# Spacing the tasks that read DMA-added weight blocks, and letting the next item's tasks go ahead

## The chip, the cores and the metric

The kernel runs on one core of a Trainium2 chip. The metric is device time in microseconds (us), the median of several executions, lower being better. TensorE is called PE in the profile, its weight loads PEld, VectorE DVE, ScalarE ACT, GpSimd POOL and SyncE SP.

## The reference

Three layers follow each other. The input is four batches of 576 tokens with 512 features.

- Attention: 8 heads of width 64, with a mask that is causal by blocks of 64 tokens.
- A mixture of 8 experts, all of them applied to all tokens: for each expert `relu(x @ w1[e]) @ w2[e]`, weighted by a router matrix `P` that is normalised over rows and columns eight times in turn. The hidden width of an expert is 1024.
- A gated layer: `(silu(x @ w_gate) * (x @ w_val)) @ w_out` with a hidden width of 1536.

All inputs and outputs are 32-bit floats; the weights of the last layer reach the kernel as pairs of words and are put together on the chip.

## The kernel before, in words

Each large product is done as seven half-size products instead of eight (a scheme of Strassen's kind), and each operand as a high and a low 16-bit part. So each weight tile of 512 by 512 needs seven operands: three are splits of its own 256-wide blocks or their negatives (W11, W21, W22), four are splits of sums of blocks (T1 to T4). The splits run on ACT (the high part, L173) and DVE (the low part, L174). The sums are not made by an engine that computes: a DMA issued from POOL adds one block onto another in place (L292).

The experts make 16 units of one w1 tile and one w2 tile each (u = 0 to 15). Units 0 and 1 run for the first token blocks beside attention; the second tile of these two needs no sums. From u = 2 on, the main stage runs one unit after the other over five token blocks (four of 256 pairs of tokens, one of 128). A unit has 63 *slots*: in each slot PE does six matmuls (or twelve of half width) of the unit's first product (`products_in`, L543) and six of a second product (`products_out`, L651) of an earlier block. The counter `clock[0]` goes up by one in each such step of `products_in`, by `tick()`, and nowhere else before the last stage.

Weights of later units are prepared in the background. An *item* is one weight tile (or, for the last layer, a quarter of one), with a list of *tasks*. `Background.step` takes the next task of the current item, if there is one and it may go. The item of a weight tile has four tasks that find block maxima (L376, with a negation on ACT at L348), an exchange of the maximum over partitions by way of PE, and then the tasks of `sum_tasks`:

- t0 splits W11. t1 finishes it, adds block 01 onto block 00 and splits W21. t2 finishes it, adds 11 onto 10 and splits W22. t3 finishes it and adds 11 onto 01.
- one `gap`, a task that does nothing
- t5 splits T1 from block 00 and adds 00 onto 10. t6 finishes it and adds 00 onto 11.
- two gaps
- t8 splits T3 from block 01. t9 splits T4 from block 10. t10 splits T2 from block 11. One more task finishes it.

In the main stage `background()` calls `step` up to twice a slot: once when the work left is over 4 tasks behind an even pace that would end at slot 58 of the unit, a second time when it is over 9 behind. A unit's items are the two tiles of the unit that follows, and a share of the last layer's quarters, in the order `share[:-2] + [i1] + share[-2:] + [i2]`. A last-layer tile is prepared in four quarter items, the fourth of which also has the sum tasks; its operands are written to DRAM for later. `bg.until((u, 0))` and `bg.until((u, 1))` run what is left of a tile at once, with `force`, when its unit's products are about to need it.

Beside attention another such object, `w0`, does units 0 and 1. There `step` is called 0.53 times for each of the three parts of an attention step, and no item is loaded ahead of the current one (`Background(0)`). The products of units 0 and 1 start there when the first batch has been through attention, in `first_part`: it calls `w0.until((0, 0))`, then the products of unit 0 on block 0 (14 half products, one for each two parts of an attention step), then `w0.finish()`, which runs all that is left of `w0` at once, then the products of unit 1.

A task's first entry is the number of buffers it needs free, or a function that says whether it may go; the maximum's exchange already used such a function.

Of the kernel before, what the change touches and what calls it, by code (L numbers as in the profile page):

```python
# [25 lines left out]
W11, W21, W22, T4, T1, T2, T3 = range(7)  # L26
# [4 lines left out]
def attention_moe_glu_kernel(  # L31
# [187 lines left out]
    clock = [0]  # L219
    places = Places(0)  # L220

    class Background:
# [14 lines left out]
        def step(self, force=False):  # L237
            self.turn += 1
            if not self.now:
                if not self.items:  # L240
                    return False
                if not self.loaded:
                    self.load(1)
                if not self.loaded or self.turn < self.loaded[0] and not force:
                    return False
                self.now.extend(self.items.popleft()[2])
                self.loaded.popleft()
            self.load(self.ahead)
            n, t, *kind = self.now[0]
            self.light = kind == [0]  # L250
            if not places.spare(n, force):
                return False
            self.now.popleft()
            if t is not None:
                t()
            if kind == [2] and not self.now and self.loaded and self.turn >= self.loaded[0]:
                n, t, *kind = self.items[0][2][0]
                if kind == [0] and places.spare(n):
                    self.loaded.popleft()
                    self.now.extend(self.items.popleft()[2])  # L260
                    self.now.popleft()
                    t()
            elif self.light and self.loaded and self.turn >= self.loaded[0]:
                tasks = self.items[0][2]
                if tasks[0][2:] == (1,) and places.spare(tasks[0][0]):
                    self.light = False
                    t = tasks.pop(0)[1]
                    if not tasks:
                        self.items.popleft()
                        self.loaded.popleft()  # L270
                    if t is not None:
                        t()
            return True

        def finish(self):
            while self.now or self.items:
                assert self.step(True), "no place left"
# [3 lines left out]
                assert self.step(True), "no place left"  # L281


    def sum_tasks(b, sp, name, flip):

        los = {}

        def add(o, x):
            nc.gpsimd.dma_start(o, x, accum_op=ALU.add)  # L292

        def up(o, src, minus=False):
            los[o] = sp(o, src, minus)

        def low(o, *gone):
            los.pop(o)()
            places.give(*gone)

        def t0():
            up(W11, b[0][0])

        def t1():
            low(W11)
            add(b[0][0], b[0][1])
            up(W21, b[1][0], True)

        def t2():
            low(W21)  # L310
            add(b[1][0], b[1][1])
            up(W22, b[1][1])

        def t3():
            low(W22)
            add(b[0][1], b[1][1])

        def t5():
            up(T1, b[0][0], True)
            add(b[1][0], b[0][0])  # L320

        def t6():
            low(T1)
            add(b[1][1], b[0][0])

        def t8():
            up(T3, b[0][1])

        def t9():
            low(T3, b[0][1])  # L330
            up(T4, b[1][0], True)
            places.give(b[0][0])

        def t10():
            low(T4, b[1][0])
            up(T2, b[1][1], flip)

        gap = (0, None, 0)
        return (
            [(1, t0, 0), (1, t1), (1, t2), (0, t3)]  # L340
            + [gap] * 1
            + [(1, t5, 0), (0, t6)]
            + [gap] * 2
            + [(1, t8, 0), (1, t9), (1, t10), (0, lambda: low(T2, b[1][1]))]
        )

    def minus(x):
# [4 lines left out]
    def expert_items(u):  # L352
# [8 lines left out]
        for i, W in enumerate((W1, W2)):  # L361
# [42 lines left out]
            if i == 1 and u < 2:  # L404

                def plain_sp(r, c, g=g, sp=sp):
                    sp((r, c), g["b"][r][c])()
                    places.give(g["b"][r][c])

                tasks += [(1, lambda r=r, c=c, f=plain_sp: f(r, c)) for r in range(2) for c in range(2)]  # L410
            else:
                tasks += sum_tasks(g["b"], sp, f"w{i}_{u}", i == 1)
# [6 lines left out]
    def glu_items(name, src, rawp):  # L419
# [66 lines left out]
        for t, r, c in quads:  # L486
            if (r, c) == (0, 0):
                b = [[None, None], [None, None]]
            cur = {}

            def last(cur=cur, b=b, r=r, c=c):
                mx(b, r, c)

            def first(cur=cur, b=b, q=(t, r, c)):
                exponent(cur, b, *q)
                if q[1:] == (1, 0):
                    minus(b[0][1])
                elif q[1:] == (1, 1):
                    minus(b[1][0])

            tasks = [(1, first, 0)]
            tasks += [(0, lambda cur=cur: (shift(cur), sign(cur))), (0, lambda cur=cur: mantissa(cur)), (0, last, 2)]
            if (r, c) == (1, 1):
                tasks[-1] = (0, lambda last=last, t=t: (last(), begin(t)))
                tasks += [(0, None, 0), (lambda force: across_made(g["r"])(force), lambda t=t: end(t))]
                tasks += sum_tasks(b, lambda o, src, minus=False, t=t: sp(t, o, src, minus), f"g{name}_{t}", name == "o")
            items.append((0, lambda cur=cur, q=(t, r, c): load(cur, *q), tasks))
# [1237 lines left out]
```

## Time and profile before

| | |
|---|---|
| time, median of 3 runs | 2194.89 us (2191.09 to 2196.18) |
| time of the profiled execution | 2203.99 us |
| its span, first to last instruction | 2202.2 us |
| PE busy | 2001.1 us, 91% |
| DVE, ACT, POOL busy | 72%, 62%, 32% |
| mean granted TensorE clock | 0.96 |
| L292, the adding DMAs | 195, of 256 KB each |

The span holds three stages: attention with units 0 and 1 up to about 385 us, the expert units up to about 1790 us, the last layer after that. An even pace of matmuls at full clock with no idle time would be the floor of the two latter. A busy PE says less than it seems, since its busy time also grows where the clock is halved.

### The profile page before, as it was taken

How to read it: one execution, taken by the hardware profiler on the slowest of the kernel's cores; microseconds unless marked ns; L12 is line 12 of the kernel's file. 1: busy time of each engine (PE TensorE's matmuls, PEld its weight loads, DVE VectorE, ACT ScalarE, POOL GpSimd, SP SyncE). 2: the span in 40 equal slices, each digit the busy share in tenths (PEclk: the TensorE clock that was granted, in tenths of full speed). 3: DMA queues.
4: the chain of work that ended last, by engine and by line, in shares of the span. 5: the costliest groups of instructions: out<-in, count | busy, mean ns of one | idle time of the engine just before them, and what ended most of it. 6: DMA issues, size and time to landing. Idle time of an engine off the chain costs nothing.

```text
span 2202.2 us, 47643 instructions
## 1 busy us (share of the span) xinstructions
PE 2001.1 (91%) x18378; PEld 1696.4 (77%) x18378; DVE 1596.5 (72%) x3583; ACT 1366.3 (62%) x2901; POOL 708.0 (32%) x1003
## 2 busy tenths in 40 slices
PE   6789899799989999898998988999888988999997
PEld 3356667688877888777887877888777887888887
DVE  6887774677777787776876767777776787666766
ACT  5666665467676677666776666677666556544442
POOL 4544343203333343333433333343333122100000
PEclk8889999899999999999999999999999999999999
DMA  6343331527887888878888797878879110210211
GB/s 170 104 121 96 106 88 48 148 54 149 173 183 151 171 158 171 185 144 174 157 167 178 145 182 146 176 148 161 186 146 202 40 45 1 57 46 17 62 40 49
DMA packets 180787, 272.22 MB, mean 124 GB/s; under 512 B 18512, under 2 KB 72784, under 8 KB 180560
## 3 DMA queue, kind: packets, MB, share of 16 engines
q0 software_dynamic: 78624, 143.17, 38.5%
q1 hardware_dynamic: 101936, 126.01, 18.7%
q8 instruction: 144, 2.36, 0.4%
q14 instruction: 83, 0.68, 0.1%
HBM read 90.98 MB, written 24.38 MB: 52 GB/s over the span
## 4 chain that ended last, share of the span: by engine, by line
PE 38%; DMA 17%; DVE 12%; issue 8%; ACT 6%; POOL 2%; POOLq 0%; ACTq 0%; DVEq 0%; SPq 0%
DMA wr<-wr 9%; PE abc_m_b L543 7%; PE m_o_b L651 6%; PE m_o_ac L651 5%; PE abc_m_c L543 3%; PE abc_v_b L543 3%; PE m_go_b L651 3%; PE abc_g_b L543 3%; PE m_go_ac L651 2%; PE abc_m_a L543 2%; DMA f_v<-f_v 2%; DMA f_g<-f_g 2%; DVE m_t L710 1%; DVE m_h L183 1%; PE abc_v_c L543 1%
## 5 line engine op out<-in xcount | busy, mean ns | idle before, releaser
L543 PEld LDWEIGHTS <-w 128*128 128x128 f16 x6720 | 620.0, 100 | 185.0 <-issue 111.4
L651 PEld LDWEIGHTS <-m_h 128*128 128x128 f16 x5292 | 521.0, 99 | 77.2 <-issue 11.6
L543 PE MATMUL abc_m_b<-xs,w 128*128 128x256 f16 (+1 forms) x3840 | 490.7, 269 | 71.5 <-DVE m_t L565 33.0
L1433 POOL DMA_DIRECT2D acc<-ev x351 | 340.4, 1098 | 549.7 <-ACT ev L1440 447.9
L651 PE MATMUL m_o_b<-w,m_h 128*128 128x256 f16 x3024 | 407.1, 274 | 5.9 <-ACT ev L1440 5.6
L651 PE MATMUL m_o_ac<-w,m_h 128*128 128x256 f16 x2268 | 320.7, 279 | 3.1 <-ACT ev L1440 3.1
L543 PE MATMUL abc_m_c<-xs,w 128*128 128x256 f16 (+1 forms) x1920 | 235.7, 267 | 22.9 <-ACT m_r L779 21.0
L173 ACT ACTIVATE w<-wr,ws 128x512 f16<-128x512 f32 x210 | 149.4, 720 | 123.1 <-DMA wr<-wr 109.0
L174 DVE SCALAR_TENSOR_TENSOR w<-wr,ws,w 128x512 f16<-128x512 f32 x210 | 156.9, 752 | 94.4 <-ACT w L173 94.1
L292 POOL DMA_DIRECT2D wr<-wr x150 | 147.5, 990 | 228.1 <-DMA wr<-wr 57.2
L1440 ACT ACTIVATE ev<-m_o_b,pe 128x256 f32<-128x256 f32 x351 | 161.6, 475 | 58.1 <-PE m_o_b L651 53.1
L183 DVE TENSOR_TENSOR m_h<-m_t,m_h 128x512 f16<-128x512 f32 (+1 forms) x210 | 132.9, 634 | 35.0 <-ACT m_h L689 34.8
L1440 ACT ACTIVATE ev<-m_o_ac,pe 128x256 f32<-128x256 f32 (+1 forms) x234 | 134.3, 579 | 36.9 <-PE m_o_ac L651 35.8
L682 ACT ACTIVATE m_h<-m_t 128x512 f16<-128x512 f32 (+1 forms) x210 | 120.5, 582 | 36.1 <-DVE m_t L580 18.5
L689 ACT CAST m_h<-m_t 128x512 f16<-128x512 f32 (+1 forms) x210 | 122.0, 581 | 16.7 <-DVE m_t L710 16.4
L686 DVE SCALAR_TENSOR_TENSOR m_h<-m_t,m_h 128x512 f16<-128x512 f32 (+1 forms) x210 | 131.1, 633 | 1.1 <-ACT m_h L682 0.7
L543 PEld LDWEIGHTS <-gg_w 128*128 128x128 f16 x1260 | 114.2, 98 | 21.4 <-issue 9.3
L1002 POOL TENSOR_SCALAR e<-e,r 128x64 f32<-128x64 f32 (+2 forms) x144 | 78.9, 555 | 159.8 <-DVE r L997 100.6
L651 PEld LDWEIGHTS <-g_h 128*128 128x128 f16 x1134 | 111.8, 99 | 19.6 <-issue 5.4
L543 PEld LDWEIGHTS <-gv_w 128*128 128x128 f16 x1260 | 114.4, 98 | 13.3 <-issue 1.2
L543 PE MATMUL abc_m_a<-xs,w 128*128 128x256 f16 (+1 forms) x960 | 119.3, 265 | 0.0
L691 POOL TENSOR_TENSOR g_h<-g_t,g_h 128x512 f16<-128x512 f32 (+1 forms) x15 | 16.0, 1069 | 250.8 <-ACT g_h L689 250.8
(319 smaller groups left out, 3454.8 us busy)
## 6 DMA issues: line engine op xcount, KB each, us to landing
acc<-ev POOLq DMA_DIRECT2D x351, 256.0 KB, 5.3
wr<-wr POOLq DMA_DIRECT2D x150, 256.0 KB, 4.0
wr<-in_w_dram SPq DMA_DIRECT2D x128, 256.0 KB, 4.7
st<-hl SPq DMA_DIRECT2D x48, 144.0 KB, 3.6
raw_g<-in_w_gate_dram SPq DMA_DIRECT2D x12, 512.0 KB, 5.1
raw_v<-in_w_val_dram SPq DMA_DIRECT2D x12, 512.0 KB, 5.4
raw_o<-in_w_out_dram SPq DMA_DIRECT2D x12, 512.0 KB, 4.8
scr_g<-gg SPq DMA_DIRECT2D x21, 256.0 KB, 3.6
```

The costliest lines, as they stand in the source:

```text
L173: nc.scalar.activation(hi, src, AF.Copy, scale=s)
L174: return lambda: nc.vector.scalar_tensor_tensor(lo, src, s, hi, op0=ALU.mult, op1=ALU.subtract)
L183: nc.vector.tensor_sub(lo, src, hi)
L292: nc.gpsimd.dma_start(o, x, accum_op=ALU.add)
L543: nc.tensor.matmul(ps[:, f], W[o][:, sh, k, f * P : (f + 1) * P], xs[:, o, mh, k, c0 : c0 + n], start=x not in begun, stop=True, skip_grou ...
L651: nc.tensor.matmul(ps, h[o][:, sh, k, ii * P : (ii + 1) * P], W[o][:, mh, k], start=o in (X11, X12) and k == 0 and j == 0, stop=True, skip ...
L682: nc.scalar.activation(hi, src, AF.Relu)
L686: nc.vector.scalar_tensor_tensor(lo, src, 0.0, hi, op0=ALU.max, op1=ALU.subtract)
L689: nc.scalar.copy(hi, src)
L1002: nc.gpsimd.tensor_scalar(et[c][:, :n], et[c][:, :n], g["r"][:, c : c + 1], 1.0, op0=ALU.mult, op1=ALU.mult)
L1433: nc.gpsimd.dma_start(acc[:, x], e, accum_op=ALU.add)
L1440: nc.scalar.activation(e[:, cols], ps, AF.Copy, scale=p)
```

## The change

Every task that reads a sum of blocks now may go only when `clock[0]` has moved on by six since the DMA that adds to its block was issued in the program (t5 waits for block 00, t8 for 01, t9 for 10, t10 for 11), unless it is forced. The three gaps go away. Where the next task of the current item may not yet go, and is one with such a function, `step` tries the first task of the next item instead, if that item has been loaded long enough, the task is not its last, and it needs no such function itself.

```diff
@@ Background.step
             if not places.spare(n, force):
-                return False
+                return callable(n) and self.ahead_of(self.items[0][2] if self.loaded and self.turn >= self.loaded[0] else ())
@@ Background
+        def ahead_of(self, tasks):
+
+            if len(tasks) < 2 or callable(tasks[0][0]) or tasks[0][1] is None or not places.spare(tasks[0][0]):
+                return False
+            n, t, *kind = tasks.pop(0)
+            self.light = kind == [0]
+            t()
+            return True
@@ sum_tasks
+    DMA_SLOTS = 6
...
+        added = {}
         def add(o, x):
             nc.gpsimd.dma_start(o, x, accum_op=ALU.add)
+            added[id(o)] = clock[0]
+
+        def summed(r, c):
+
+            return lambda force: (force or clock[0] >= added[id(b[r][c])] + DMA_SLOTS) and places.spare(1)
...
-        gap = (0, None, 0)
         return (
             [(1, t0, 0), (1, t1), (1, t2), (0, t3)]
-            + [gap] * 1
-            + [(1, t5, 0), (0, t6)]
-            + [gap] * 2
-            + [(1, t8, 0), (1, t9), (1, t10), (0, lambda: low(T2, b[1][1]))]
+            + [(summed(0, 0), t5, 0), (0, t6)]
+            + [(summed(0, 1), t8, 0), (summed(1, 0), t9), (summed(1, 1), t10), (0, lambda: low(T2, b[1][1]))]
         )
```

## Rows read from the trace of the kernel before

**Rows 1.** Page, chain of work that ended last, shares of the span by line.

```profile
DMA wr<-wr 9%; PE abc_m_b L543 7%; PE m_o_b L651 6%; PE m_o_ac L651 5%; PE abc_m_c L543 3%; PE abc_v_b L543 3%; PE m_go_b L651 3%; PE abc_g_b L543 3%; PE m_go_ac L651 2%; PE abc_m_a L543 2%; DMA f_v<-f_v 2%; DMA f_g<-f_g 2%; DVE m_t L710 1%; DVE m_h L183 1%; PE abc_v_c L543 1%
```

**Rows 2.** Waits, 481.61 to 1710.91 us: total us, times, longest.

```profile
ACT w L173 <- DMA wr<-wr: 103.9, 66, 4.1
PEld L543 <- issue: 93.6, 55, 5.8
...
ACT go L173 <- DMA f_o<-f_o: 20.1, 10, 4.9
...
ACT gg L173 <- DMA f_g<-f_g: 20.0, 11, 4.7
...
ACT gv L173 <- DMA f_v<-f_v: 18.6, 9, 4.7
```

**Rows 3.** Windows: units 2, 3, 5, 8, 10, 12 of thirteen, and all.

```profile
core 0: us, PE busy (x) PEld busy (x) DVE busy (x) ACT busy (x) POOL busy (x), PEclk, DMA share, GB/s
481.61:569.59 87.98, 83.69 (x798) 74.26 (x796) 67.08 (x138) 70.26 (x141) 32.94 (x38) 1.00 0.76 146
569.59:663.10 93.51, 85.94 (x798) 75.39 (x797) 70.43 (x139) 64.55 (x131) 35.84 (x42) 0.96 0.86 174
...
763.09:847.27 84.18, 83.54 (x806) 75.15 (x806) 67.27 (x139) 63.98 (x129) 32.88 (x38) 1.00 0.82 157
...
1041.13:1125.67 84.54, 83.68 (x806) 75.15 (x806) 67.33 (x139) 64.11 (x129) 32.91 (x38) 1.00 0.82 158
...
1222.51:1327.57 105.06, 90.68 (x802) 77.94 (x800) 73.41 (x151) 66.52 (x135) 36.72 (x42) 0.94 0.81 166
...
1426.89:1514.05 87.16, 85.14 (x806) 76.05 (x806) 67.35 (x139) 64.20 (x129) 32.94 (x38) 0.98 0.78 151
...
481.61:1710.91 1229.30, 1127.59 (x10423) 990.39 (x10421) 909.85 (x1836) 853.10 (x1713) 458.67 (x526) 0.97 0.83 165
```

**Rows 4.** Timeline of ACT in unit 9: start, duration, [idle before <- releaser].

```profile
1153.89 0.72 ACT L173 ACTIVATE gv<-f_v,gs_v 128x512 f16<-128x512 f32 x1 [1.27 <-DMA f_v<-f_v]
...
1160.35 0.72 ACT L173 ACTIVATE gv<-f_v,gs_v 128x512 f16<-128x512 f32 x1 [2.05 <-DMA f_v<-f_v]
1163.05 0.72 ACT L173 ACTIVATE gv<-f_v,gs_v 128x512 f16<-128x512 f32 x1 [1.98 <-DMA f_v<-f_v]
```

**Rows 5.** Timeline of PE just after.

```profile
1165.55 1.44 PE L543 MATMUL abc_m_b<-xs,w 128*128 128x256 f16 x6 [3.68 <-ACT abc_m_a L560]
1166.78 1.48 PE L651 MATMUL m_o_ac<-w,m_h 128*128 128x256 f16 x6
...
1171.71 0.82 PE L651 MATMUL m_o_b<-w,m_h 128*128 128x256 f16 x6
```

**Rows 6.** Timeline of POOL in the same sum: adds of t1, t3, t5, t6.

```profile
1150.38 0.86 POOL L292 DMA_DIRECT2D f_v<-f_v  x1 [1.25 <-DVE gv L174]
...
1154.40 0.86 POOL L292 DMA_DIRECT2D f_v<-f_v  x1 [0.81 <-DMA f_v<-f_v]
1157.10 0.86 POOL L292 DMA_DIRECT2D f_v<-f_v  x1 [1.84 <-DMA f_v<-f_v]
1160.94 0.86 POOL L292 DMA_DIRECT2D f_v<-f_v  x1 [2.98 <-PE abc_m_c L543]
```

**Rows 7.** Page, DMA issues: count, size, median us from issue to landing.

```profile
wr<-wr POOLq DMA_DIRECT2D x150, 256.0 KB, 4.0
```

**Rows 8.** Timeline of ACT beside attention: splits of T1 (u = 0), then u = 1.

```profile
38.72 0.72 ACT L173 ACTIVATE w<-wr,ws 128x512 f16<-128x512 f32 x1
...
122.02 0.72 ACT L173 ACTIVATE w<-wr,ws 128x512 f16<-128x512 f32 x1
...
143.93 0.72 ACT L173 ACTIVATE w_(0, 0)_1720<-wr,ws 128x512 f16<-128x512 f32 x1 [6.58 <-DVE ws L391]
```

**Rows 9.** Timeline of PE there: the first expert product, and around the finish.

```profile
109.64 1.21 PE L543 MATMUL abc_m_b<-xs,w 128*128 128x256 f16 x6
...
141.82 0.79 PE L110 MATMUL w_a<-w_d,ones 128*128 128x128 f32 x2 [5.64 <-DVE w_d L103]
```

**Rows 10.** Timeline of DVE there: last block maxima and last low part.

```profile
139.39 1.86 DVE L376 TENSOR_REDUCE wmx<-wr 128x1 f32<-128x512 f32 x3
...
146.68 0.75 DVE L174 SCALAR_TENSOR_TENSOR w_(1, 1)_1729<-wr,ws,w_(1, 1)_1729 128x512 f16<-128x512 f32 x1
```

**Rows 11.** Windows: the stretch ahead of the finish.

```profile
0.00:137.40 137.40, 101.29 (x659) 54.79 (x659) 104.76 (x340) 81.21 (x222) 66.87 (x155) 0.84 0.53 138
```

## The prediction, as made before the run

> **What bounds the kernel now.** First the chain of waits of the page: the largest share of one line is not a matmul but the transfer that adds one weight block onto another, 9% of the span, with the last layer's adds (f_v, f_g) behind it [rows 1]. The chain counts transfers that hide as well, so next comes the list of waits of the expert units. There ACT stands 162.6 us ahead of its split (L173) for these adds: 103.9 for expert tiles, 20.1, 20.0 and 18.6 for the last layer's [rows 2]. PE's weight loads are idle for 93.6 us in the same stretch, under "issue": no releaser is shown, so it has to be found in a timeline.
>
> Unit 9 shows it. ACT waits 2.05 us for a sum, does T3, waits 1.98 us for the next [rows 4]. PE, whose finished banks ACT has to empty, stands for 3.68 us, and its next group of six matmuls takes 1.44 us, where six take 0.82 as shown (overlapping with the next group) from 1171.71 on [rows 5]. So PE's clock was at the lower of its two levels, 1.2 GHz, after the stop and back at 2.4 some 5 us later. A stall costs about its length and half as much again.
>
> The windows by unit say how much it all is. Units 5 and 8 take 84.18 and 84.54 us with PE busy for 83.5 of them at full clock: this is the floor of 63 slots. Units 2 and 12 take 87.98 and 87.16. All thirteen take 1229.30, so the other nine take 1229.30 - 343.86 = 885.4, or 98.4 each [rows 3]. These nine prepare three sums (the two tiles and a last-layer tile), the four light ones two. More tasks in 58 slots means two steps a slot, and then four steps between t1 and t5 are only two or three slots. A slot is 84.18 / 63 = 1.34 us. So what can be won is at most 9 x (98.4 - 84.2) = 128 us, all of it in the heavy units.
>
> **The change, main stage.** Six slots are 8.0 us. Against that stand the adds: 4.0 us from issue to landing in the median [rows 7], and more than one in a row. In unit 9 the add of t3 goes out 4.0 us after that of t1 (it writes the block that t1's add still reads), t5's waits for t2's, and t6's goes out at 1160.94, 10.6 us after t1's [rows 6]. Taken reader by reader:
>
> - T1 needs t1's add: ready 3.5 us after it (1153.89), allowed after 8.0. No wait left.
> - T3 needs t3's add: ready 10.0 us after t1's (1160.35). t3 is issued at least one slot after t1, so T3 comes 9.4 us or more after t1, and the add of t1 leaves POOL up to about 1 us after its slot. What remains is 0 to 1.6 us.
> - T4 and T2 need the adds of t5 and t6, which now go out 8 us after t1 with their blocks ready, but t6's still behind t3's landing. With 4 us each they are there 13 to 15 us after t1, and asked for at 16 us or later. No wait left.
>
> So I count nearly all the 162.6 us of ACT's waits as gone, and what is left of them (up to 1.6 us at T3) as too short to stop PE, since in units 5 and 8 ACT gets by. What is late next is the last tile of a unit: a sum now spans 14 slots, three of them 42, with exchanges and maxima about 60 to 64 of a unit's 63. It may run some five slots into the next unit, which needs that tile only about 18 slots in (14 for its first block, four of lag). The tasks let ahead (four maxima, or three steps of a quarter) fill part of the blocked slots. But work is bunched: two splits in a slot are 1.4 us of ACT and 1.5 of DVE [rows 8, 10] in 1.34 us, on top of the unit's own work; DVE is 67 to 73 us busy in a unit [rows 3], so it fits on the mean, and not in every slot. Waits for raw loads and exchanges stay.
>
> Heavy units then lie between 86 us (floor and about 2 us of what is no sum's) and 93 (half of the loss found again in bunching). I take 89.5, nearer the floor, since the light units reach it with the same kinds of tasks: 885.4 - 9 x 89.5 = **80 us less**; the bounds give 111 and 48. Light units: nothing, their adds are spaced already. Removed gaps cost no engine anything; the queue of SP gets nothing new; on POOL, the adds of the units' outputs queue behind an add that waits, as now.
>
> DMA is where a limit may stand. Its share times the length is 747 us for the heavy units (0.83 x 1229.3 less 273 of the light ones), 83 per unit [rows 3]; at 89.5 us that is a share of 0.93, above the 0.86 that any unit shown has had.
>
> **The change, attention.** `clock[0]` stands still until the first expert product, at 109.64 us [rows 9]. T1 of unit 0 was split at 38.72 [rows 8]; now t5 blocks there, no item is loaded ahead, and `w0` does nothing for 70 us. Three prices:
>
> - `until((0, 0))` at about 108 us runs t5 to t10 at once. T4 and T2 wait for adds issued moments before, 4 to 5 us; ACT also does four splits there that it did earlier. I take +4 us (2 to 6).
> - 14 half products give about 15 calls of `step`: enough for the second tile of unit 0 (4 calls for its load, 11 tasks) and nothing more. So `finish()`, which now runs only the end of the last tile (the split at 143.93 after 6.58 us without work for ACT, PE idle for 5.64), must run unit 1's first tile from load to T2, and then the second. Its maxima end at 141.25 as the other tile's do now [rows 10], its first split is at 143.9; the low part 0.75, t1's add 4.0, t3's add behind it 4.0, t6's behind that 4.0, T2 and its low part 1.5: about 158.5. Then DVE may take the second tile: four maxima 2.5 (1.86 for three), the exchange 2.7 (141.25 to 143.93 [rows 8, 10]), four splits with the last low part 3.5: 167 instead of 147.4, where the last low part ends now [rows 10]. +20 us, since ACT and DVE serve attention in the same order (17 to 24).
> - Gained ahead of it: some 14 reductions and low parts of about 0.7 us, 10 us of DVE, and 8 us of ACT leave the stretch up to 110 us. DVE is busy for 104.76 of 137.4 us there, no engine is full [rows 11], so perhaps half shows: -6 (0 to -11).
>
> Together **+18 us** (8 to 30).
>
> **Sum.** 2203.99 - 80 + 18 = 2142 against the profiled execution. That one is 9.1 us above the median, so in the median's terms 2194.89 - 62 = **2133 us**, 2.8% less.
>
> One rule speaks against the gain. The Trainium skill, "DMA: Bandwidth & Descriptors", section "Anatomy of one DMA — SWDGE (gpsimd) path", gives a DMA issued by GpSimd 2.0 us and its bytes over 436 GB/s, which is an estimate of 2.6 us for 256 KB. By it two adds in a row land in 5.2 us, old gaps nearly cover them, and the sum would be about +18 alone; by the rows (4.0 in the median) it is -62. The median of 150 adds decides against it here.
>
> **Rivals.**
>
> - *The adds are not what stops PE.* Then the spacing wins nothing, attention's price stays: 2195 + 18 = 2213. It would be so if adds landed within the present spacing. ACT's 162.6 us against it [rows 2], and the stop in unit 9 that begins inside such waits [rows 4, 5]. The quoted section of the Trainium skill leads there. Chance 0.03.
> - *The DMA engines become the bound*, the one that can end slower. If no unit gets past a share of about 0.9 without adds landing later than six slots, heavy units stay at 83 / 0.9 = 92 us or more; at 0.86 it is 96.5, a gain of 17, and attention's 18 decides: 2196. So above 96.4 us per heavy unit the change is slower. For it: shares of 0.82 to 0.86 now. Against it: adds are spread wider, which shortens their queue. 2165 to 2210. Chance 0.14 (0.07 faster, 0.03 same, 0.04 slower).
> - *The heavy units reach the floor* (86 us or less, -111 us) and attention hides more (+10): 2094, or 2080 to 2105. Units 5 and 8 speak for it, bunching against. Chance 0.12.
> - *It hardly acts*: the new wait rarely differs from the old spacing, since blocked tasks are forced or done late anyway. 2185 to 2200. Light units show that spacing alone matters, so 0.05 (0.02 faster, 0.02 same, 0.01 slower).
>
> **How the numbers follow.** The forecast has the remaining 0.66; its own range is 2105 to 2165. A measurement of this kernel tells 0.2%, 4.4 us, from no change. Faster: 0.66 + 0.12 + 0.07 + 0.02 = 0.87. Same 0.05. Slower 0.04 + 0.03 + 0.01 = 0.08. The range goes from the upper bound of the gain with little price, -111 + 10, so 2094, to the lower with a full one, -48 + 30, so 2177, and leaves out some 0.07 below and 0.12 above.
>
> **What would show it.** Right: ACT's waits at L173 for the adds fall from 162.6 to under 40 us; heavy units at 87 to 92 us, light ones within 2 of now; granted clock of the units at 0.99; DMA share of heavy units above 0.9; POOL's adds of t5 some 8 us after t1's. In attention no split of T1 for unit 0 before about 105 us, and a gap of 25 to 30 us around 137 to 167 in which ACT and DVE only prepare weights. Wrong: waits at L173 that stay at T3 and T2 with landings of 7 us and more; new stops of PE behind two splits in one slot, or behind a forced tile at the start of a unit; attention's end later by over 30 us.

## The result, and the profile after

The changed kernel takes 2173.81 us (median of 4 runs, 2171.44 to 2177.77), the kernel before, run beside it, 2193.26 (2191.09 to 2196.18): a ratio of 0.9914, with a 95% interval of 0.9897 to 0.9931. So 19.5 us are won, where 62 had been forecast. The direction was right and the time lies inside the range of 2094 to 2177, but the gain is a third of the one predicted.

The two traces differ by more, 2202.2 to 2170.3 us of span, because the profiled execution of before lay some 10 us above its median. A second profile of before (experiment k) has a span of 2196.5. Both are in this table. The units are measured from one start of the scaling of router weights (L1412 of before, L1427 of after) to the next.

| kernel | unit 2 sets out | units 2 to 14 | what follows | span |
|---|---|---|---|---|
| before | 481.6 | 1229.3 | 491.3 | 2202.2 |
| before, second profile | 480.8 | 1226.3 | 489.4 | 2196.5 |
| after | 493.3 | 1188.4 | 488.6 | 2170.3 |

So the units won 38 to 41 us, and 12 were lost ahead of them, in attention. The lines of the functions moved: L173 and L174 are where they were, L292 of before is L305, L376 is L391, L543 is L558, L651 is L666.

From the page of after: the chain by line, and DMA issues (count, size, median us from issue to landing). The adds are 3% of the chain now, 9% before [rows 1], but one takes longer, 4.9 us against 4.0 [rows 7].

```profile
PE abc_m_b L558 11%; PE m_o_b L666 11%; PE m_o_ac L666 8%; PE abc_m_c L558 5%; DMA wr<-wr 3%; PE abc_m_a L558 3%; PE abc_v_b L558 3%; PE abc_g_b L558 3%; PE m_go_b L666 3%; PE m_go_ac L666 2%; DMA wr<-in_w_dram 1%; PE abc_v_c L558 1%; PE abc_g_c L558 1%; DVE m_t L725 1%; PE m L621 1%
...
wr<-wr POOLq DMA_DIRECT2D x150, 256.0 KB, 4.9
```

Waits of after, 493.31 to 1681.75 us (total us, times, longest). They answer to [rows 2]: ACT stands for the adds 36.4 + 5.8 + 5.5 + 2.3 = 50.0 us instead of 162.6, and PE's idle weight loads fall by less, from 93.6 to 55.2. The block maxima on DVE wait 13.2 us for weights that have not been loaded yet (10.4 in the kernel before, with a longest of 2.4).

```profile
PEld L558 <- issue: 55.2, 27, 6.6
ACT w L173 <- DMA wr<-wr: 36.4, 32, 2.5
DVE wmx L391 <- DMA wr<-in_w_dram: 13.2, 10, 3.3
...
ACT gg L173 <- DMA f_g<-f_g: 5.8, 3, 2.2
ACT go L173 <- DMA f_o<-f_o: 5.5, 4, 2.3
...
ACT gv L173 <- DMA f_v<-f_v: 2.3, 1, 2.3
```

Windows of after: units 3, 4 and 5, and all thirteen, with the columns of [rows 3]. The light units are 2, 5, 8 and 11 now, 86.0 and three times 84.3 to 84.8. The nine heavy ones take the rest, (1188.4 - 339.4) / 9 = 94.3 us each, where 98.4 was before and 89.5 forecast. Unit 11 is light in place of 12 because the quarters of the last layer are shared out to the units by their number of tasks, and a gap counted as a task. Without the gaps unit 11 gets no last-layer sum and unit 12 gets one: 10 and 15 adds are issued in these two, 15 and 11 before. The sums of all units together are the same, so that their total can be compared; a single unit can't always be.

```profile
579.31:672.00 92.69, 85.59 (x790) 75.44 (x789) 67.72 (x134) 65.36 (x129) 36.54 (x42) 0.96 0.89 181
672.00:767.90 95.90, 88.16 (x813) 77.33 (x811) 74.01 (x151) 67.55 (x135) 34.97 (x40) 0.96 0.84 169
767.90:852.20 84.30, 84.30 (x815) 76.01 (x813) 67.75 (x142) 64.42 (x130) 34.09 (x39) 1.00 0.81 156
...
493.31:1681.75 1188.44, 1113.04 (x10432) 990.00 (x10431) 908.64 (x1838) 861.00 (x1713) 457.11 (x524) 0.98 0.85 169
```

Three kinds of stops of PE in the heavy units are shown here; a fourth, of 2.69 us in the last block of units 4, 7 and 10, is taken up under i. The first is a sum that six slots do not cover. This is the timeline of unit 3 (start, duration, [idle before <- releaser]): POOL's adds of t1, t3, t5 and t6, then the splits of T1, T3, T4 and T2 on ACT, then DVE and PE.

```profile
605.25 0.86 POOL L305 DMA_DIRECT2D f_g<-f_g  x1 [2.65 <-DVE gg L174]
...
611.16 0.86 POOL L305 DMA_DIRECT2D f_g<-f_g  x1 [3.96 <-DMA f_g<-f_g]
...
613.31 2.26 POOL L305 DMA_DIRECT2D f_g<-f_g  x1
...
615.09 2.25 POOL L305 DMA_DIRECT2D f_g<-f_g  x1
...
612.69 0.71 ACT L173 ACTIVATE gg<-f_g,gs_g 128x512 f16<-128x512 f32 x1
615.63 0.71 ACT L173 ACTIVATE gg<-f_g,gs_g 128x512 f16<-128x512 f32 x1
621.37 0.72 ACT L173 ACTIVATE gg<-f_g,gs_g 128x512 f16<-128x512 f32 x1 [1.58 <-DMA f_g<-f_g]
625.01 0.72 ACT L173 ACTIVATE gg<-f_g,gs_g 128x512 f16<-128x512 f32 x1 [2.04 <-DMA f_g<-f_g]
...
625.77 0.75 DVE L174 SCALAR_TENSOR_TENSOR gg<-f_g,gs_g,gg 128x512 f16<-128x512 f32 x1 [2.89 <-ACT gg L173]
...
627.17 1.03 PE L558 MATMUL abc_m_b<-xs,w 128*128 128x256 f16 x6 [2.66 <-DVE m_t L580]
```

T1 and T3 find their sums done, and t5's add goes out 8.1 us after t1's, as forecast. But that add is there only when T4 is released, 8 us after its issue, and t6's some 10 us after its own. ACT waits 1.58 and 2.04 us. DVE's low part stands 2.89 us for ACT's split, the `m_t` that releases PE comes right behind it on DVE, and PE stops for 2.66.

The second kind is an exchange of the maximum that stands behind tasks let ahead. DVE and PE in unit 10:

```profile
1256.89 1.27 DVE L391 TENSOR_REDUCE wmx<-wr 128x1 f32<-128x512 f32 x2
...
1259.89 1.27 DVE L391 TENSOR_REDUCE wmx<-wr 128x1 f32<-128x512 f32 x2
...
1262.86 0.28 DVE L116 TENSOR_REDUCE gv_r<-m_gv 128x1 f32<-128x128 f32 x1
...
1256.62 0.46 PE L110 MATMUL m_gv<-gv_d,ones 128*128 128x128 f32 x2 [2.34 <-DVE gv_d L103]
...
1263.20 0.80 PE L110 MATMUL m_w<-w_d,ones 128*128 128x128 f32 x2 [3.50 <-DVE gv_r L116]
```

PE has spread the maximum of the gv tile by 1257.1. Since the exchange too has a function for an entry, the maxima of the next tile (wmx), twice two of them, go ahead while it is awaited, and even that tile's exchange on PE (m_w). On DVE, gv_r stands behind all of these and the unit's own work and begins at 1262.86; m_w is released by it, and PE stands for 3.50 us.

The third kind is a maximum that begins before its own load has landed. DVE, ACT and PE in unit 6: three of four maxima wait for the transfer, ACT's negation waits for a maximum, `m_r` stands behind the negations on ACT, and PE, which `m_r` releases, stands for 4.25 us. The waits of the maxima are not new (10.4 us before, 7.4 in experiment a, where nothing is let ahead).

```profile
902.30 0.69 DVE L391 TENSOR_REDUCE wmx<-wr 128x1 f32<-128x512 f32 x1 [1.20 <-DMA wr<-in_w_dram]
903.86 0.69 DVE L391 TENSOR_REDUCE wmx<-wr 128x1 f32<-128x512 f32 x1 [0.87 <-DMA wr<-in_w_dram]
...
906.91 0.69 DVE L391 TENSOR_REDUCE wmx<-wr 128x1 f32<-128x512 f32 x1 [1.18 <-DMA wr<-in_w_dram]
...
904.58 0.63 ACT L363 ACTIVATE wr<-wr 128x512 f32<-128x512 f32 x1 [2.63 <-DVE wmx L391]
...
906.94 0.94 PE L558 MATMUL abc_m_c<-xs,w 128*128 128x128 f16 x12 [4.25 <-ACT m_r L794]
```

In attention both things happened that the prediction had named, an earlier start and a late finish. Timeline of PE and ACT in after: the first expert product at 87.94 (109.64 before, [rows 9]), the burst of `until` with its waits for adds, and the gaps of `finish`.

```profile
87.94 0.83 PE L558 MATMUL abc_m_b<-xs,w 128*128 128x256 f16 x6
...
97.39 0.88 PE L1049 MATMUL t<-ident,e 128*128 128x128 f32 x3 [7.27 <-ACT a L1050]
...
134.28 0.80 PE L110 MATMUL w_a<-w_d,ones 128*128 128x128 f32 x2 [7.12 <-DVE w_d L103]
153.56 0.77 PE L110 MATMUL w_a<-w_d,ones 128*128 128x128 f32 x2 [18.48 <-DVE w_d L103]
...
93.53 0.72 ACT L173 ACTIVATE w<-wr,ws 128x512 f16<-128x512 f32 x1 [3.77 <-DMA wr<-wr]
96.16 0.72 ACT L173 ACTIVATE w<-wr,ws 128x512 f16<-128x512 f32 x1 [1.91 <-DMA wr<-wr]
```

### The profile page after: what moved, and what is told of

It is laid out like the page before. It is cut to its first block, busy times and chain, and to the rows that moved or that the text cites. A ratio compares the mean times of both kernels' runs of the same rounds, so it can differ in the third digit from the quotient of the medians.

```text
span 2170.3 us, 47700 instructions
## 1 busy us (share of the span) xinstructions
PE 1969.9 (91%) x18378; PEld 1687.0 (78%) x18378; DVE 1594.1 (73%) x3583; ACT 1374.1 (63%) x2901; POOL 706.2 (33%) x1003
## 4 chain that ended last, share of the span: by engine, by line
PE 54%; DVE 12%; DMA 7%; ACT 5%; issue 3%; POOL 1%; SPq 0%; ACTq 0%; POOLq 0%; DVEq 0%
PE abc_m_b L558 11%; PE m_o_b L666 11%; PE m_o_ac L666 8%; PE abc_m_c L558 5%; DMA wr<-wr 3%; PE abc_m_a L558 3%; PE abc_v_b L558 3%; PE abc_g_b L558 3%; PE m_go_b L666 3%; PE m_go_ac L666 2%; DMA wr<-in_w_dram 1%; PE abc_v_c L558 1%; PE abc_g_c L558 1%; DVE m_t L725 1%; PE m L621 1%
## 5 line engine op out<-in xcount | busy, mean ns | idle before, releaser
L558 PEld LDWEIGHTS <-w 128*128 128x128 f16 x6720 | 618.5, 100 | 135.5 <-issue 65.7
L666 PEld LDWEIGHTS <-m_h 128*128 128x128 f16 x5292 | 519.7, 99 | 72.5 <-issue 10.1
L558 PE MATMUL abc_m_b<-xs,w 128*128 128x256 f16 (+1 forms) x3840 | 482.5, 266 | 34.8 <-DVE m_t L580 21.0
L1448 POOL DMA_DIRECT2D acc<-ev x351 | 333.2, 1104 | 487.7 <-ACT ev L1455 332.3
L666 PE MATMUL m_o_b<-w,m_h 128*128 128x256 f16 x3024 | 411.0, 276 | 8.0 <-ACT ev L1455 4.5
L666 PE MATMUL m_o_ac<-w,m_h 128*128 128x256 f16 x2268 | 312.5, 274 | 0.0
L558 PE MATMUL abc_m_c<-xs,w 128*128 128x256 f16 (+1 forms) x1920 | 236.1, 267 | 19.0 <-ACT m_r L794 15.9
L305 POOL DMA_DIRECT2D wr<-wr x150 | 146.9, 1000 | 252.1 <-DMA wr<-wr 74.9
L174 DVE SCALAR_TENSOR_TENSOR w<-wr,ws,w 128x512 f16<-128x512 f32 x210 | 156.1, 750 | 75.6 <-ACT w L173 75.2
L173 ACT ACTIVATE w<-wr,ws 128x512 f16<-128x512 f32 x210 | 148.7, 718 | 76.9 <-DMA wr<-wr 50.6
L183 DVE TENSOR_TENSOR m_h<-m_t,m_h 128x512 f16<-128x512 f32 (+1 forms) x210 | 132.9, 634 | 13.1 <-ACT m_h L704 12.4
L558 PEld LDWEIGHTS <-gg_w 128*128 128x128 f16 x1260 | 113.6, 98 | 20.9 <-issue 9.4
L666 PEld LDWEIGHTS <-g_h 128*128 128x128 f16 x1134 | 111.1, 99 | 19.0 <-issue 5.4
L558 PEld LDWEIGHTS <-gv_w 128*128 128x128 f16 x1260 | 113.9, 98 | 13.5 <-issue 1.7
L558 PE MATMUL abc_m_a<-xs,w 128*128 128x256 f16 (+1 forms) x960 | 120.3, 266 | 0.0
L580 DVE TENSOR_TENSOR m_t<-m_t,abc_m_b 128x512 f32<-128x512 f32 (+1 forms) x80 | 50.4, 630 | 77.0 <-PE abc_m_b L558 65.5
```

The lines of the kernel that those rows point to most:

```text
L173: nc.scalar.activation(hi, src, AF.Copy, scale=s)
L174: return lambda: nc.vector.scalar_tensor_tensor(lo, src, s, hi, op0=ALU.mult, op1=ALU.subtract)
L183: nc.vector.tensor_sub(lo, src, hi)
L558: nc.tensor.matmul(ps[:, f], W[o][:, sh, k, f * P : (f + 1) * P], xs[:, o, mh, k, c0 : c0 + n], start=x not in begun, stop=True, skip_grou ...
L666: nc.tensor.matmul(ps, h[o][:, sh, k, ii * P : (ii + 1) * P], W[o][:, mh, k], start=o in (X11, X12) and k == 0 and j == 0, stop=True, skip ...
L1448: nc.gpsimd.dma_start(acc[:, x], e, accum_op=ALU.add)
```

## The experiments

All times are medians beside runs of the kernel before on the same chip, whose own median lay between 2193.3 and 2196.0 us; with intervals of the ratios of 0.0014 to 0.0025 to either side, differences between two changed kernels are good to some 5 us. The expectations number their theories anew each time and say what each is. In short, the accounts of the missing 43 us were: tasks let ahead get in the way on DVE; the spacing itself is too short or too long; the DMA engines are the bound; attention costs more than counted.

**a. The spacing alone.** Nothing is let ahead.

```diff
-                return callable(n) and self.ahead_of(self.items[0][2] if ... else ())
+                return False
```

> The wait of six slots stays, no task of the next item is let ahead. Theory 1 (the tasks let ahead give back what the spacing wins: block maxima stand on DVE before the exchange that PE waits for): the three stops of PE of 2.4 to 3.8 us at the exchange in each of units 4, 7 and 10 fall back to about 1 us, those units from 96 to 97.6 us to about 90, the whole to 2140 to 2160. Theory 2 (the spacing makes three sums too long for a unit, and the tasks let ahead are what lets them fit): tiles are forced at the start of units, heavy units at 97 us or more, 2185 and up. Theory 3 (the DMA engines bound the heavy units): no change, 2168 to 2180.

2194.1 us against 2196.0, a ratio of 0.9993 (0.9979 to 1.0007): no gain. ACT's wait for `wr` at L173 is only 27.5 us in the units, and the units still take 1210.4, since blocked slots stay empty: the light units 5 and 8 rise to 88.9 and 91.9 us, and tiles are forced at the start of three units, where PE stops 3.9 to 4.2 us. So three quarters of the waits at the splits go (41.5 us are left of 162.6), but the units win only 16 to 19 us, and attention takes 10 to 11 of them (unit 2 sets out at 491.7): it is the letting ahead that makes room for the spacing.

**b. The old list in attention.** Until the main stage begins, the tasks and gaps of before are used.

```diff
+        if not soon[0]:
+            gap = (0, None, 0)
+            return (
+                [(1, t0, 0), (1, t1), (1, t2), (0, t3), gap, (1, t5, 0), (0, t6), gap, gap]
+                + [(1, t8, 0), (1, t9), (1, t10), (0, lambda: low(T2, b[1][1]))]
+            )
```

> The tiles prepared beside attention (units 0 and 1) keep the old list with its gaps, all others have the change. The changed trace is 11.7 us behind the one before when unit 2 sets out. If that is the forced tile of unit 1 less what attention gains ahead of it, and nothing later hangs on it: 2174 - 11 = 2163 (2158 to 2167), unit 2 sets out at 481 to 484 us. If the later start is made good in the units anyway: 2171 to 2176.

2159.5 us, a ratio of 0.9837 (0.9814 to 0.9861), 14.3 under the changed kernel. Unit 2 sets out at 482.7 instead of 493.3, which is 10.6 of them. This is the price of attention, forecast as 18.

**c. More time between a load and the first tasks of its item,** let ahead or not.

```diff
-                self.loaded.append(self.turn + (4 if self.ahead else 4))
+                self.loaded.append(self.turn + (10 if self.ahead else 4))
```

> An item's tasks may begin ten calls of step after its load is issued, not four. Theory 1b (steps now come two to a slot, four calls are two slots, less than a load takes; DVE then stands at block maxima for data): the stops of PE of 4.4 to 6.6 us behind such maxima in units 6, 9 and 13 go, 15 to 25 us less, 2150 to 2160. Theory 3 (DMA engines as the bound) and theory 2 (a unit has too few slots): no gain or a loss, 2172 to 2185.

2172.3 us, a ratio of 0.9895 (0.9874 to 0.9916): like the changed kernel. The maxima's waits for loads go (0.8 us are left), and tiles that come late take their place: the units sum to 1189.0, with stops of up to 10 us where a tile is forced at the start of a unit, and ACT's wait for `wr` rises to 65.1. The stops behind loads are real in the trace, but this cure costs as much.

**d. Ahead only of a sum's tasks, not of the exchange.**

```diff
-                return callable(n) and self.ahead_of(self.items[0][2] if ... else ())
+                return getattr(n, "of_sum", False) and self.ahead_of(self.items[0][2] if ... else ())
...
-            return lambda force: (force or clock[0] >= added[id(b[r][c])] + DMA_SLOTS) and places.spare(1)
+            def may(force):
+                return (force or clock[0] >= added[id(b[r][c])] + DMA_SLOTS) and places.spare(1)
+            may.of_sum = True
+            return may
```

> Tasks go ahead only while a sum is awaited, not while the maximum's exchange is. Theory 1: PE's stops of 2.4 to 3.8 us at the exchange fall to about 1 us, 10 to 20 us less, 2155 to 2165. If those stops come of DVE's load as a whole and not of the maxima let ahead at that place: within 4 us of 2174.

2161.4 us, a ratio of 0.9837 (0.9815 to 0.986), 12.4 under the changed kernel, 8.5 of it in the units (1179.9). The stops of PE at exchanges in the units fall from 16.9 to 6.5 us. So the exchange behind maxima, shown above in unit 10, was worth some 12 us.

**e and f. No adds at all**, in the kernel before and in the changed one. Both leave out the 195 adding transfers, so that T1 to T4 are splits of single blocks; order and waits of the programs stay.

```diff
-            nc.gpsimd.dma_start(o, x, accum_op=ALU.add)
```

> The kernel before, with the 195 adding DMAs left out: the four operands T1 to T4 of each tile are split from single blocks instead of sums. It measures what all waiting for adds was worth. If that is the loss of the heavy units, as the prediction took it (98.4 us down to the floor of 84.2 and 2 to 5 us more): heavy units at 86 to 89.5, 2196 - 80 to 2196 - 115, so 2081 to 2116. If raw loads, exchanges and two tasks a slot make the heavy units long by themselves: heavy units at 92 to 95, 2135 to 2165.

> The changed kernel with the 195 adding DMAs left out, the order of all tasks and their waits of six slots kept (T1 to T4 are split from single blocks). Theory 3 (the DMA engines bound the heavy units): without a quarter of the DMA work of a unit they fall to 86 to 88 us, 2174 - 60, so 2100 to 2125. Theory 2 (slots and bunching, not transfers): heavy units stay at 91 to 94, 2150 to 2168.

e takes 2081.8 us, a ratio of 0.9482 (0.9469 to 0.9495), f 2121.7, 0.9667 (0.9651 to 0.9683). Windows of e, unit 4 and all units, with the columns of [rows 3]:

```profile
644.66:731.13 86.47, 84.96 (x813) 75.79 (x811) 72.50 (x149) 66.27 (x135) 23.32 (x27) 1.00 0.68 147
...
473.05:1593.60 1120.55, 1091.54 (x10423) 975.76 (x10421) 908.05 (x1836) 855.07 (x1713) 301.30 (x349) 1.00 0.66 140
```

And the same two of f:

```profile
653.60:748.20 94.60, 88.01 (x813) 77.50 (x811) 73.85 (x151) 67.55 (x135) 23.36 (x27) 0.96 0.63 136
...
480.72:1630.80 1150.08, 1103.04 (x10431) 985.14 (x10430) 908.28 (x1838) 861.63 (x1713) 303.03 (x351) 0.99 0.64 136
```

This splits the units' gain. In the order of before the adds cost 1229.3 - 1120.5 = 108.8 us, which is all that could be won. In the new order they still cost 1188.4 - 1150.1 = 38.3, and the new order by itself, with no add in sight, costs 1150.1 - 1120.5 = 29.6. 108.8 - 38.3 - 29.6 = 40.9; this sum comes out by the way it is made, and what is measured are its terms. Of the 29.6 us, 18.0 are idle time of PE and 11.5 longer busy time, at a granted clock of 0.99 for 1.00.

The time of f lies in the band of theory 3, that of the DMA engines (2100 to 2125), but its heavy units do not agree with it. Five take 85.0 to 88.3 us; units 4, 7, 10 and 13 take 91.7 to 94.6, unit 4 with a DMA share of only 0.63, so full DMA engines are not what holds these. Since f takes away the waits for adds and the adds' load on the DMA engines at once, it can't tell how the 38.3 us divide between the two.

**g. Four slots in place of six.**

```diff
-    DMA_SLOTS = 6
+    DMA_SLOTS = 4
```

> The change with a wait of four slots (5.4 us) for six. Theory 2 (three sums of 14 slots do not fit a unit's 63): shorter sums (10 slots) win more than the longer waits at T3 lose, 2155 to 2168. Theory of the prediction (six slots are needed to cover two adds in a row): ACT's waits at L173 double from some 60 us, heavy units 2 to 3 us longer, 2185 to 2200.

2213.7 us, a ratio of 1.008 (1.0059 to 1.0102): slower than before, and slower than either theory had it. The units take 1225.8 us, as before the change; what is lost lies ahead of them, where unit 2 sets out at 497.9. Waits of g, 475 to 1730 us:

```profile
ACT w L173 <- DMA wr<-wr: 136.2, 52, 5.6
PEld L558 <- issue: 84.2, 46, 4.8
...
ACT gg L173 <- DMA f_g<-f_g: 19.2, 8, 3.9
ACT gv L173 <- DMA f_v<-f_v: 17.7, 7, 4.3
ACT go L173 <- DMA f_o<-f_o: 15.0, 8, 4.1
```

Four slots are 5.4 us at the prediction's 1.34 us a slot. The waits at the splits are back at 188 us. 101 of them are at T3 (told by the order of a tile's splits), whose add goes out behind that of t1. So the chained adds need the two slots more, as the prediction read them. The Trainium skill, "DMA: Bandwidth & Descriptors", section "Anatomy of one DMA — SWDGE (gpsimd) path", gave the prediction its estimate of 2.6 us for one add; by it, two in a row would be covered here. The trace does not agree: the median of one `wr` add is 4.8 us in the units of g and 5.2 in those of after, and none took less than 3.2.

**h. b and d together.**

> Both parts that gave time by themselves: the old lists for the tiles beside attention, and tasks let ahead only while a sum is awaited. If they touch different stages, their gains add, 14 and 12 us: 2148 (2143 to 2153). If the start of unit 2 sets how the units run: 2155 to 2162.

2139.4 us (2136.6 to 2146.9), a ratio of 0.9749 (0.9731 to 0.9767): the fastest of all, 34 us under the changed kernel. 14.3 + 12.4 would be 26.7. By the ratios b and d are each 0.0077 under the changed kernel and h is 0.0165, so that the two gains add as well as these runs can tell. In the traces some of the rest lies ahead of unit 2, which sets out at 475.2. There b, as the changed kernel, still has a long stop of PE at an exchange that was let ahead while its tile's maxima waited for their load. This is the one of b:

```profile
406.42 0.80 PE L110 MATMUL m_w<-w_d,ones 128*128 128x128 f32 x2 [12.41 <-DVE w_d L103]
```

In h the exchange of that tile comes later, with no wait, and 5.88 us are left at a matmul behind one such maximum (6.42 in the kernel before):

```profile
402.16 2.08 PE L568 MATMUL abc_m_b<-xs,w 128*128 128x256 f16 x9 [5.88 <-DVE m_t L590]
...
418.14 0.39 PE L110 MATMUL m_w<-w_d,ones 128*128 128x128 f32 x2
```

**i. h without its adds**, as f is the changed kernel without them.

> The version with attention's old list and with tasks let ahead at the sums alone (the exchange excepted), and without its 195 adding transfers (T1 to T4 are splits of single blocks; waits and order stay). The changed kernel without its adds kept 29.6 us in its units over the kernel before without adds, most of it in units 4, 7 and 10 (94.5 us each). Theory 1, that this is the exchange standing behind maxima let ahead: the units fall by about as much as they did with the adds (12 us), from 1150 to some 1138, and the whole to about 2095. Theory 2, that it is the order at the sums (blocked tasks go later, so the last half-width block of these units is bunched): the three units stay within 2 us of 94.5, the units' sum within 5 of 1150, the whole about 2107 from attention's 14 us alone.

2100.4 us, a ratio of 0.956 (0.9539 to 0.9582). The units take 1143.1, 7.0 under f, neither the 12 of the one theory nor under the 5 of the other; units 4, 7 and 10 are at 92.2, 92.2 and 90.5 instead of some 94.5. So the exchange explains a quarter of the 29.6, at most, since i also has b's list and b's units had come out 3.2 shorter. In i's units eight stops of PE of over 2 us are left, 24.4 us together, against two of 4.8 in e. Four, in units 3, 6, 9 and 13 (3.0 to 4.0 us), stand behind maxima that wait for their loads, as above in unit 6. The other four, of 2.6 to 2.7 us, are in the last blocks of units 3, 4, 7 and 10, and the timeline of i shows for unit 4 what is ahead of one on DVE: low parts of the gg tile follow those of the w tile (three each in 10 us), among the work of the last half-width block, and `m_t` at L589, for which PE stands, is late.

```profile
704.44 0.75 DVE L174 SCALAR_TENSOR_TENSOR gg<-f_g,gs_g,gg 128x512 f16<-128x512 f32 x1
706.00 0.75 DVE L174 SCALAR_TENSOR_TENSOR gg<-f_g,gs_g,gg 128x512 f16<-128x512 f32 x1 [0.82 <-ACT gg L173]
706.67 0.41 DVE L589 TENSOR_TENSOR m_t<-m_t,abc_m_b 128x256 f32<-128x256 f32 x1
...
707.14 0.83 PE L567 MATMUL abc_m_b<-xs,w 128*128 128x128 f16 x12 [2.69 <-DVE m_t L589]
```

**j. h with eight slots.**

> The same version with its adds, and a distance of eight slots in place of six. Theory 1, that the waits of ACT left at the splits (about 40 us in all) are adds that land between six and eight slots after their issue: these waits halve at least and the whole gains 5 to 12 us against 2139, 2127 to 2134. Theory 2, that what is left comes from order and bunching, so that a longer sum pushes more tasks to the end of a unit or over it: the waits fall little or tiles are forced at the start of units, and the whole is 2140 to 2165.

2174.4 us, a ratio of 0.99 (0.9877 to 0.9924), 35 us above h and above the band of the second theory too. ACT's waits at L173 for the last layer's adds go (1.8 us, 19.6 in h), but that for `wr` does not fall (37.0 us, 30.9 in h), it moves. The timeline of j at the start of unit 5, ACT and PE:

```profile
749.43 0.72 ACT L173 ACTIVATE w<-wr,ws 128x512 f16<-128x512 f32 x1 [3.77 <-DMA wr<-wr]
751.98 0.72 ACT L173 ACTIVATE w<-wr,ws 128x512 f16<-128x512 f32 x1 [1.82 <-DMA wr<-wr]
...
754.25 1.44 PE L676 MATMUL m_o_b<-w,m_h 128*128 128x256 f16 x6 [10.47 <-ACT ev L1465]
```

A tile that is not ready when its unit begins is forced, with waits for adds issued moments before, and PE stands for 10.47 us; three more units (8, 11 and 14) begin so, with stops of 9.9 to 11.1 us. So six slots lie between two steep sides: with four the adds are not there, with eight the tile isn't.

**k. The kernel before, profiled once more.**

> The kernel before, profiled once more, since its first profiled execution lay 9 us above its median. If the difference lies in a single stretch, the units' sum of 1229 us or the attention's part should be the one that differs by about 9 us; if the execution as a whole was slower, all stretches share it by their length (about 0.4%).

2198.25 us. Its units take 1226.3, 3.0 less than in the first profile, what follows 1.9 less, attention 0.8: the difference is spread over all stretches.

## Why the prediction was wrong

**The units, -80 forecast, -38 to -41 measured.** This is the term that failed, and in it the step "Taken reader by reader", with its "No wait left" for T4 and T2, for which the adds of t5 and t6 were taken at 4 us each. The heavy units were to lie between 86 and 93 us and came to 94.3, outside both bounds. Without any add the new order takes 90.1 of them (f), near the 89.5 of the forecast, which was meant with adds that hide: 0.6 us a unit, 5 in all. The other 4.2 us a unit, 38 in all, are what the adds still cost.

- That the adds bound the heavy units was right, and so was the ceiling: 108.8 us without adds (e), where the prediction had at most 128 and an upper bound of 111. Without adds the heavy units of before take (1120.5 - 339.5) / 9 = 86.8 us; the rival of the floor named 86 or less.
- The adds did not take 4 us each. That median was taken over `wr` alone, 150 of the 195 adds, and over all steps of a sum, as they fell in the order of before; the other 45 had medians of 5.1 to 6.6 us even there (f_g, f_v, f_o). By steps the units of before have medians of 3.4 us for the add of t1, 4.6 and 4.4 for those of t2 and t3, but 6.3 and 5.7 for those of t5 and t6; in unit 9, which the prediction read, the adds of t3 and t5 took 5.9 each (T3 and T4 begin as they land, [rows 4, 6]). In the units of after t5's and t6's have 6.4 and 5.3, with longest ones of 10.5 and 9.9 where six slots are 8.0, and two adds issued 1.8 us apart beside four output adds took 8 and 10 (unit 3, above, with a DMA share of 0.96 in 604 to 627 us). So T4 and T2 still wait, 31.6 us, and T3 16.8 in thirteen waits of up to 2.4, where "0 to 1.6" was said; it is 50.0 us at the splits in all instead of "under 40", and the stops are not too short: 2.66 us of PE behind a wait of 2.04 of ACT. All that is left of the adds' cost is 38.3 us (after less f).
- The bunching was named, and bounded by "half of the loss found again". The 89.5 that was taken is the middle of 86 and 93, not "nearer the floor", and leaves it 3.5 us a unit above 86. It is 29.6 us without any add (f less e), or 3.3 a heavy unit: the heavy units of f take (1150.1 - 339.4) / 9 = 90.1 us, so this term was about right in size, though only in part for the reason given (two splits in a slot). That `ahead_of` works at the exchange as well, where the old code already put a function, was in the diff's text, and its consequence was not seen: 12 us of the whole (d), and up to 7 of the 29.6 (i less f). The other 22.6 us are seen in the trace of i, at maxima ahead of their loads and in the last half-width blocks, but no run settles what each is worth, and c did not win from the former.
- "Removed gaps cost no engine anything" left out that the gaps counted in the sharing of the last layer's quarters, so that another unit is light. What that is worth no run shows.

**Attention, +18 forecast, +12 measured ahead of unit 2, 14 by experiment b.** The sum was near by luck: its terms were off by 16 and 9 us in opposite directions. Windows of the stretch ahead of the first expert product, in after

```profile
0.00:87.94 87.94, 65.43 (x466) 33.52 (x466) 65.61 (x238) 53.32 (x160) 48.83 (x123) 0.94 0.49 134
```

and in before:

```profile
0.00:109.60 109.60, 78.14 (x470) 39.18 (x470) 79.92 (x275) 61.25 (x173) 52.25 (x126) 0.81 0.52 137
```

"Gained ahead of it" was -6 and is -21.7. The work left out was 14.3 us of DVE and 7.9 of ACT, near the 10 and 8 counted, but PE's clock stood at 0.94 instead of 0.81 with it, and PE was busy 12.7 us less for nearly the same matmuls. All traces agree on the gain, and less on the clock: with the new list (after, a, c, d, f, g) the first expert product comes at 87.9 to 91.1 us and the clock of the stretch is 0.89 to 0.98, with the old one (before, b, e, h, i, j, k) at 103.5 to 110.0 and 0.81 to 0.85. But g, with the highest clock of 0.98, is the latest of the first group, so the share of the clock in the 21.7 us is not shown. Against that, from the first expert product to the end of the last low part it is 71.2 us instead of 37.8, +33.4 where the two bursts were counted as 24. The gaps of the finish are 7.12 and 18.48 us, 25.6 as "25 to 30" said, and the last split comes at 157.49; the low part after it ends at 159.13, where 167 was forecast (the first tile's steps add up to 158.2 there, not 158.5). Without adds the new list still puts unit 2 back by 7.6 us (480.7 in f, 473.1 in e). The granted clock was 0.54 from 126 to 159 us.

**Of what was to show it right:** the light units within 2 us and the spacing of t5 (8.1 us in unit 3) came so; ACT's waits (50.0), the heavy units (94.3), their DMA share (0.81 to 0.91, above 0.9 in one only) and the clock (0.98 for 0.99) did not reach it. What had been named as wrong signs, landings of 7 us and more and stops behind bunched splits, is what the trace shows.

**The rivals.** That adds are not what stops PE is refuted by e. That the change hardly acts is refuted by the waits, 50.0 us for 162.6. That the heavy units reach the floor does not hold: they are at 90.1 us even without adds (f). The heavy units' mean of 94.3 lies in the band of the rival of full DMA engines (92 to 96.5), but f has long units at a share of 0.63, so it is not a bound for all of them; that it lengthens the landings inside them (8 and 10 us at a share of 0.96) is what the trace suggests, and no run took it alone.

**The sum.** Between the two profiles -41 + 12 - 3 = -32 us; from the second profile of before -26; in medians -19.5. The time lies in the range by luck: the gain of the units is below its lower bound of 48, and the range paired that bound with a price of attention of 30, where 12 to 14 came. The kernel before spread from 2192.3 to 2202.6 in the seven runs beside i, j and k, which is more than its first three had shown.

## What to carry to other kernels

A transfer's median over all of its places is no size for the place that counts: take it step by step, and in the trace at hand. A wait that is taken away by spacing needs a task to put in its place, and a task that is pushed over the end of a span can cost more than the wait did (here with eight slots): measure the spacing from both sides. When tasks may overtake others, ask at each place where the condition can fire, not only at the one it was written for, what the overtaking task puts ahead in the queues of the engines. And take away the suspected cost altogether, before and after the change: the two runs split a small net gain into what was won, what was left and what was given back.

## What the runs showed of the hardware

- One and the same kind of add of 256 KB took from 3.2 to 10.5 us to land, with a median of 4.2 in the kernel before (longest 9.0) and 5.2 after (all 195 of each), though nothing changed in the add itself. The longest shown here (8 and 10 us, unit 3) fall where the DMA share is 0.96. Stores of `scr_g` of the same size went from a median of 3.6 us before to 5.4 after; without adds it is 3.4 in the order of before (e) and 2.2 in the new one (f), so the order counts as well as the load.
- With 14 us less of DVE's work beside attention, the first expert product came 21.7 us earlier, and the granted clock of PE in that stretch stood at 0.94 instead of 0.81. That the one follows from the other is not shown.
- A stop of PE cost more than its length: e, against the kernel before, has 72.7 us less idle time in the units and 36.1 us less busy time for as many matmuls, at a granted clock of 1.00 for 0.97.
